# The second MLP's products as seven of quarters instead of eight, with the weights' sums formed during the first MLP

## The chip, the cores and the metric

The kernel runs on 1 core of one Trainium2 chip. The metric is device time in microseconds (us), the median of several executions. TensorE (PE) multiplies, VectorE (DVE), ScalarE (ACT) and GpSimd (POOL) do elementwise work, and SyncE (SP) issues the DMA transfers.

## The reference

```python
def _moe_ref(x, w_in, w_out, s, b):          # first MLP
    h = x @ w_in
    r = np.maximum(h, 0.0)
    return (s * (r * r) + b) @ w_out

def _moe2_ref(x, w_in, w_out):               # second MLP, beta = 1
    h = x @ w_in
    g = np.where(h >= 1, h, np.where(h <= -1, 0.0, (h + 1) ** 2 / 4))
    return g @ w_out

x = _attn_ref(q, k, v)   # 4 batches, 8 heads, 576 positions of 64; 4 heads local (32 back), 4 strided (every 32nd)
x = x.transpose(0, 2, 1, 3).reshape(2304, 512)
return _moe2_ref(_moe_ref(x, ...), ...)      # both MLPs: 512 -> 2048 -> 512
```

## The kernel before

Attention runs in 38 tiles (`attend`): scores on PE, mask and row maximum on DVE (L366), exponentials on ACT (L376), the division by the row sum (L383), a transpose (L392), the product with v (L404, L408). What it gives is written as a pair of tiles, `xh` (rounded to the matmul's type) and `xl` (the remainder).

Both MLPs are tiled alike. Tokens come in five units of 512, 448, 448, 448 and 448; the 2048 hidden rows in two halves (`hf`) of eight blocks of 128 (`m`). For each layer, half, unit and block, `hidden` multiplies four chunks of the input by a weight block into one PSUM bank `h`, and `output`, two steps later (`LAG`), adds four products into the PSUM banks `acc`. A step is thus 24 matmuls, since every product is done as three (`mm3`: high by high, high by low, low by high; L451 to L453). Between the two lies the nonlinearity, in the second MLP L487 (ACT), L488 and L490 (DVE), and the split of its result into `gh` (L258, ACT) and `gl` (L492, POOL). The sums of the first half go to DRAM (`part`) and come back for the second half.

Weights come as 64-bit floats, 512 KB for one of 64 blocks; four DVE instructions (L287 to L293) decode them, and L296 on POOL makes the low part. They lie in `w0h`, `w0l`, `w1h`, `w1l`, and six blocks of each layer's second half go into tiles that attention has left.

No engine decides the order at run time. `Issue.order` is a planner: it gives each operation a due time from back to front, and then takes the one that can start first on its costs, ties by due time. Operations with two possible engines have two entries; in the kernel before, DVE is charged 0.07 more there (`SPARE`). "port" in an entry keeps DVE and POOL from being planned at once.

## Time and profile before

| | us |
|---|---|
| median of 3 runs (910.68 to 911.11) | 911.03 |
| the profiled execution | 909.68 |
| its span, first to last instruction | 907.9 |
| PE busy in the span (98%) | 888.9 |
| first matmul of the first MLP | 33.57 |
| first matmul of the second MLP | 498.65 |
| last matmul starts | 903.76 |

The profiled execution lasted 1.78 us longer than its span. A matmul's busy time of 0.36 us overlaps its neighbours: the pace is read from start to start. The first 24 matmuls of 448 columns behind 498.65 still belong to the first MLP (its last two steps).

### The profile page before, as it was taken

What the parts mean: (1) busy time and instruction counts of PE and PEld (TensorE: products, weight loads), DVE (VectorE), ACT (ScalarE), POOL (GpSimd) and SP (SyncE); (2) the same over time, 40 slices, a digit from 0 to 9 for tenths busy, and PEclk for the clock granted to TensorE, in tenths of its full rate; (3) what the DMA queues carried; (4) which work ended last, traced back from release to release, by engine and by line L of the source; (5) the groups of instructions that cost most, each with busy time, mean ns of one, the idle gap of its engine ahead of it and who ended that gap; (6) DMA issues with size and microseconds to landing.
All of it is one profiled execution on the core that took longest, in us unless ns stands there. A gap on an engine that the chain in (4) does not pass through costs nothing.

```text
span 907.9 us, 12795 instructions
## 1 busy us (share of the span) xinstructions
PE 888.9 (98%) x4670; PEld 783.8 (86%) x4670; DVE 437.4 (48%) x990; ACT 411.3 (45%) x936; POOL 368.5 (41%) x329
## 2 busy tenths in 40 slices
PE   7899999999999999999999999999999999999998
PEld 4677789889989888999999888999999889999997
DVE  5988923333247676621147787233267523323232
ACT  6877745555445556544354445233244422222221
POOL 2565642333236656542446565222235422222221
PEclk9999999999999999999999999999999999999999
DMA  9666442322214433110303234011132102012021
GB/s 330 206 207 205 143 140 84 114 65 85 91 44 136 134 97 106 47 41 1 110 12 123 69 96 137 1 42 39 49 110 93 64 1 87 31 52 82 1 82 41
DMA packets 37502, 81.63 MB, mean 90 GB/s; under 512 B 4160, under 2 KB 19520, under 8 KB 37440
## 3 DMA queue, kind: packets, MB, share of 16 engines
q1 hardware_dynamic: 37440, 80.82, 27.8%
q8 instruction: 37, 0.61, 0.3%
q14 instruction: 25, 0.20, 0.1%
HBM read 66.64 MB, written 14.16 MB: 89 GB/s over the span
## 4 chain that ended last, share of the span: by engine, by line
PE 91%; ACT 3%; DVE 3%; POOL 1%; issue 1%; DMA 1%; SPq 0%; POOLq 0%; ACTq 0%
PE acc L451 15%; PE h L451 15%; PE h L452 14%; PE h L453 14%; PE acc L452 14%; PE acc L453 14%; ACT sm L376 2%; PE side L392 1%; PE side L357 1%; PE side L404 1%; PE side L408 1%; PE side L353 1%; DVE dt L293 1%; DMA w1h<-in_strd 1%; DVE sm L366 1%
## 5 line engine op out<-in xcount | busy, mean ns | idle before, releaser
L492 POOL TENSOR_TENSOR gl<-t,gh 128x448 fp32r<-128x448 f32 (+1 forms) x160 | 200.6, 1254 | 392.9 <-ACT gh L258 315.4
L451 PE MATMUL h<-xh,w0h 128*128 128x448 f32 (+1 forms) x460 | 175.5, 382 | 0.0
L451 PE MATMUL acc<-gh,w1h 128*128 128x448 f32 (+1 forms) x460 | 173.4, 377 | 0.5 <-ACT po L258 0.5
L452 PE MATMUL h<-xl,w0h 128*128 128x448 f32 (+1 forms) x460 | 171.2, 372 | 0.0
L453 PE MATMUL h<-xh,w0l 128*128 128x448 f32 (+1 forms) x460 | 171.1, 372 | 0.0
L452 PE MATMUL acc<-gl,w1h 128*128 128x448 f32 (+1 forms) x460 | 169.9, 369 | 0.0
L453 PE MATMUL acc<-gh,w1l 128*128 128x448 f32 (+1 forms) x460 | 169.7, 369 | 0.0
L258 ACT ACTIVATE gh<-t 128x448 fp32r<-128x448 f32 (+1 forms) x160 | 94.1, 588 | 139.8 <-DVE t L490 106.1
L488 DVE SCALAR_TENSOR_TENSOR t<-t 128x448 f32<-128x448 f32 (+1 forms) x80 | 54.9, 686 | 197.4 <-ACT t L487 197.3
L487 ACT ACTIVATE t<-h,half_t 128x448 f32<-128x448 f32 (+1 forms) x80 | 51.7, 646 | 148.4 <-PE h L453 148.3
L484 DVE TENSOR_SCALAR t<-t,fix_t 128x448 f32<-128x448 f32 (+1 forms) x80 | 51.0, 638 | 136.3 <-ACT t L479 118.2
L451 PEld LDWEIGHTS acc<-gh,w1h 128*128 128x128 f32 x460 | 86.3, 188 | 11.1 <-issue 1.0
L453 PEld LDWEIGHTS h<-xh,w0l 128*128 128x128 f32 x460 | 86.6, 188 | 10.5 <-POOL w0l L296 0.6
L451 PEld LDWEIGHTS h<-xh,w0h 128*128 128x128 f32 x460 | 86.7, 188 | 10.4 <-issue 0.5
L475 ACT ACTIVATE t<-h 128x448 f32<-128x448 f32 (+1 forms) x80 | 44.4, 555 | 112.5 <-PE h L453 111.4
L453 PEld LDWEIGHTS acc<-gh,w1l 128*128 128x128 f32 x460 | 86.2, 187 | 10.4
L452 PEld LDWEIGHTS h<-xl,w0h 128*128 128x128 f32 x460 | 86.8, 189 | 9.2
L452 PEld LDWEIGHTS acc<-gl,w1h 128*128 128x128 f32 x460 | 86.4, 188 | 8.5
L376 ACT ACTIVATE sm<-sm,mx 128x96 f32<-128x96 f32 (+2 forms) x152 | 56.1, 372 | 20.5 <-DVE mx L366 20.4
L293 DVE SCALAR_TENSOR_TENSOR dt<-raw,dt 128x512 int32<-128x512 int32 x64 | 64.0, 1003 | 0.6
L291 DVE SCALAR_TENSOR_TENSOR dt<-raw,dt 128x512 int32<-128x512 int32 x64 | 57.5, 898 | 0.6
L490 DVE TENSOR_TENSOR t<-h,t 128x448 f32<-128x448 f32 (+1 forms) x80 | 50.8, 635 | 2.0
(95 smaller groups left out, 1336.7 us busy)
## 6 DMA issues: line engine op xcount, KB each, us to landing
raw<-in_w_ins SPq DMA_DIRECT2D x32, 512.0 KB, 4.1
raw<-in_w_outs SPq DMA_DIRECT2D x32, 512.0 KB, 3.6
part<-po SPq DMA_DIRECT2D x32, 224.0 KB, 2.2
...
qv<-in_loc SPq DMA_DIRECT2D x18, 256.0 KB, 2.7
kb<-in_loc SPq DMA_DIRECT2D x15, 256.0 KB, 3.5
kb<-in_strd SPq DMA_DIRECT2D x15, 256.0 KB, 3.5
...
```

Source lines behind the costliest of these rows:

```text
L258: e.activation(out=out, in_=in_, func=AF.Copy)
L291: op(lambda e: e.scalar_tensor_tensor(out=t.tile, in0=words(1), scalar=-0x40000000, in1=t.tile, op0=ALU.bitwise_and, op1=ALU.bitwise_or), ...
L293: op(lambda e: e.scalar_tensor_tensor(out=t.tile, in0=words(0), scalar=29, in1=t.tile, op0=ALU.logical_shift_right, op1=ALU.bitwise_or), [ ...
L376: e.activation(out=sm.tile[0:nq, a, 0:nk], in_=sm.tile[0:nq, a, 0:nk], func=AF.Exp, scale=-1.0, bias=mx.tile[0:nq, a:a + 1], accum_out=dn. ...
L451: e.matmul(out=acc, lhsT=wh, rhs=ah, start=first, stop=False)
L452: e.matmul(out=acc, lhsT=wh, rhs=al, start=False, stop=False)
L453: e.matmul(out=acc, lhsT=wl, rhs=ah, start=False, stop=last)
L484: op(lambda e: e.tensor_scalar(out=c(t), in0=c(t), scalar1=sb_t[:, 0:1], scalar2=sb_t[:, 1:2], op0=MUL, op1=ADD), [dve2(n, 0.0007)], [fix_ ...
L487: op(lambda e: e.activation(out=c(t), in_=c(p), func=AF.Relu, scale=0.5, bias=half_t), [act(n)], [p], [t])
L488: op(lambda e: e.scalar_tensor_tensor(out=c(t), in0=c(t), scalar=1.0, in1=c(t), op0=ALU.min, op1=MUL), [dve2(n)], (), [t])
L490: op(lambda e: e.tensor_tensor(out=c(t), in0=c(p), in1=c(t), op=ALU.max), [dve(n)], [p], [t])
L492: op(lambda e: e.tensor_tensor(out=c(gl), in0=c(t), in1=c(gh).bitcast(F32), op=SUB), [pool(n)] + [dve2(n)], [t, gh], [gl])
```

## The change

The second MLP is no longer made of steps. Tokens come in three pairs of two 384-token tiles. A product of a weight matrix with a pair is taken as a 2 by 2 product of quarters: weights A11 to A22 (the contraction halved, the output halved), inputs B11 to B22 (the contraction halved, the two token tiles). Seven products (`PRODS`) of quarters or sums of quarters give the four results: weights A11, A12, A22 and S1 to S4, inputs B11, B21, B22 and T1 to T4.

The weights' sums are made once by `prepare` during the first MLP, 16 times: two 512 KB blocks are decoded, four sums of 256 columns formed, seven matrices split into high and low parts, and eight DMAs write these to DRAM (`dw`). Six of the 16 come in the first MLP's first half. In the second MLP every block loads one matrix (256 KB, `wmat`) and does six matmuls of 384 columns with it. `w0h` and `w0l` hold 16 such matrices.

For each pair, `inputs` forms T1 to T4 in place in the first MLP's output (`x2`, held in the freed `xh` tiles) and splits the seven inputs. `hidden2` does 4 groups of 14 blocks, each for two blocks of 128 hidden rows in both halves; products are added into banks that hold earlier ones, and `evacuate` copies or adds (L745) between them. Then come the nonlinearity (L758, L759, L761) and `output2`: for each of the seven products 8 blocks, whose input is a quarter of the nonlinearity's result or a sum made in place (L806) and is split just ahead into `gh` (ACT) and `gl` (L812), three buffers deep. Partial sums in DRAM are no longer needed in the second MLP.

The planner loses `SPARE`; now an entry is charged what it is slower than the operation's fastest engine. Attention's operations are pulled forward (`AHEAD`), and its loads, the weights' and others keep their order as lines.

```diff
--- before.py
+++ after.py
...
+AHEAD = 3.3
...
-BUFS = {"kb": KB, "qv": QV, "sm": SM, "pt": PT}
-SPARE_TAGS = [(("kb", "kb"), ("qv", "sm")), (("kb", "kb"), ("sm", "sm")), (("qv", "qv"), ("pt", "pt"))]
+BUFS = {"kb": KB, "qv": QV - 1, "qx": 1, "sm": SM - 1, "sx": 1, "pt": PT}
+SPARE_TAGS = {(0, 0): ("kb", "kb"), (0, 1): ("kb", "kb"), (1, 0): ("qx", "sx")}
...
+NP = 384
+PAIRS = NT // (2 * NP)
+KP = DFF // 256
+
+PRODS = ((1, "A11", "B11"), (5, "S1", "T1"), (6, "S2", "T2"), (3, "S4", "B22"), (7, "S3", "T3"), (2, "A12", "B21"),
+         (4, "A22", "T4"))
+WMAT = {"A11": 0, "A12": 1, "A22": 2, "S2": 3, "S4": 4, "S3": 5, "S1": 6}
+
+SUMS = {"T1": ("B11", "B12", "B11"), "T2": ("B11", "B22", "B11"), "T3": ("B12", "B22", "B12"), "T4": ("B21", "B21", "B11")}
+EARLY = 6
+CP = 9
+G_TAGS = ["kb"] * 4 + ["qv", "qv", "qx", "sx"] + ["sm"] * 2 + ["pt"] * 2 + ["pi"] * 4 + ["w1h", "w1l"] * 8
 SPACE_A, SPACE_W = 2.6, 2.4
-SPARE = 0.07
...
-                    key = (at + (SPARE if e == "dve" and len(o.engs) > 1 else 0.0), o.due, o.n, d, at)
+                    key = (at + d - min(x[1] for x in o.engs), o.due, o.n, d, at)
...
+    def prepare(o, i):
+
+        begin = len(plan.ops)
+        src = w_outs if o else w_ins
+        at = o * KP + i
+        tag = ("qv", "sm")[at % 2]
+        d1, d2 = (buf(sp, tag, [128, DM], I32, BUFS[tag]) for _ in range(2))
+        _, x1, _, load = decode(src[2 * MS + i], lasts if at < EARLY else [*lasts, chain[0]], [d1, d2], d1)
+        _, x2, *_ = decode(src[2 * MS + KP + i], [load], (), d2)
+        where = {"A11": (d1, x1, 0), "A22": (d2, x2, 1)}
+        where.update({"A21": (d1, x1, 1), "A12": (d2, x2, 0)} if o else {"A12": (d1, x1, 1), "A21": (d2, x2, 0)})
+
+        def parts(b, f, k, names):
+            n, q = 256 * len(names), [WMAT[name] for name in names]
+            qs = slice(q[0], q[-1] + 1, max(q[-1] - q[0], 1))
+            hi = buf(sp, "pt", [128, 512], F32R, PT)
+            lo = buf(sp, "pi", [128, 512], F32R, KD) if at < EARLY else buf(sp, "po", [128, 512], F32R, PO)
+            x = lambda: f()[:, k * 256:k * 256 + n]
+            op(lambda e: copy(e, hi.tile[:, 0:n], x()), [act(n)], [b], [hi], allocs=[lo],
+               line=pi_line if at < EARLY else None)
+            op(lambda e: e.tensor_tensor(out=lo.tile[:, 0:n], in0=x(), in1=hi.tile[:, 0:n].bitcast(F32), op=SUB),
+               [pool(n), dve2(n)], [b, hi], [lo])
+            for w, y in enumerate((hi, lo)):
+                op(lambda e, y=y, w=w: e.dma_start(
+                    out=dw[o][i][qs, :, w, :].rearrange("q p n -> p q n"),
+                    in_=y.tile[:, 0:n].bitcast(F32).rearrange("p (q n) -> p q n", n=256)), [dma(n * 512)], [y],
+                   part=[dw_buf[o][i][v] for v in q])
+
+        for names in [("A11",), ("A12", "A22")] if o else [("A11", "A12"), ("A22",)]:
+            parts(*where[names[0]], names)
+
+        for name, l, r, how in (("A22", "A21", "A22", ADD), ("A21", "A11", "A21", SUB), ("A11", "A22", "A11", SUB),
+                                ("A12", "A12", "A11", SUB)):
+            (b, f, k), (bl, fl, kl), (br, fr, kr) = (where[v] for v in (name, l, r))
+            h = lambda f, k: f()[:, k * 256:(k + 1) * 256]
+            op(lambda e, f=f, k=k, fl=fl, kl=kl, fr=fr, kr=kr, how=how: e.tensor_tensor(
+                out=h(f, k), in0=h(fl, kl), in1=h(fr, kr), op=how), [dve2(256), pool(256)],
+               [v for v in dict.fromkeys((bl, br)) if v is not b], [b])
+        for names in [("S2", "S3"), ("S4", "S1")] if o else [("S2", "S4"), ("S3", "S1")]:
+            parts(*((d1, x1) if names[0] == "S2" else (d2, x2)), 0, names)
+        prepared.extend(plan.ops[begin:])
...
+    def inputs(p):
+        t0 = {f"B{k}{t}": (2 * p + t - 1) * NP for k in (1, 2) for t in (1, 2)}
+        ks = lambda b: slice(0, 2) if b[1] == "1" else slice(2, 4)
+        x = lambda b, u, a, n: x2[u].tile[:, ks(b), a:a + n]
+        for i, (_, _, name) in enumerate(PRODS):
+            place = name
+            if name in SUMS:
+                place, l, r = SUMS[name]
+                cuts = sorted({0, NP} | {d for b in (place, l, r) for _, _, d, _ in span(t0[b], NP)})
+                todo = []
+                for c0, c1 in zip(cuts, cuts[1:]):
+                    f = {b: next(span(t0[b] + c0, c1 - c0))[:2] for b in {place, l, r}}
+                    todo.append((f, c1 - c0))
+
+                def sums(e, todo=todo, place=place, l=l, r=r):
+                    for f, n in todo:
+                        e.tensor_tensor(out=x(place, *f[place], n), in0=x(l, *f[l], n), in1=x(r, *f[r], n), op=SUB)
...
+                op(sums, [("dve", 0.07 * len(todo) + 2 * NP * 0.00104, 0.1, "port"),
...
+                whole = lambda w, d, n, b=b: b.tile[:, w, :, d:d + n]
+                hi = [lambda d=d, n=n, f=whole: f(0, d, n) for _, _, d, n in pieces]
+                lo = [lambda d=d, n=n, f=whole: f(1, d, n) for _, _, d, n in pieces]
+                n = len(pieces)
+                op(lambda e, src=src, hi=hi: [copy(e, h(), s()) for s, h in zip(src, hi)],
+                   [("act", 0.17 * n + 2 * NP * 0.00062, 0.1)], [quarter[p][place]], [b], after=[x_last[i], *prepared])
+                op(lambda e, src=src, hi=hi, lo=lo: [e.tensor_tensor(out=l(), in0=s(), in1=h().bitcast(F32), op=SUB)
+                                                     for s, h, l in zip(src, hi, lo)],
+                   [("pool", 0.1 * n + 2 * NP * 0.0022, 0.1, "port"), ("dve", 0.07 * n + 2 * NP * 0.00104, 0.1, "port")],
+                   [quarter[p][place]], [b])
             else:
-                got = x_buf[u][c]
-                op(lambda e, y=y, c=c: copy(e, xh[u][:, c, :], y.tile[:, 0:n]), [act(n)], [y], [got])
-                op(lambda e, y=y, c=c: e.tensor_tensor(out=xl[u][:, c, :], in0=y.tile[:, 0:n],
...
+    def wmat(o, i, name):
+        tag = ("w0h", "w0l")[loads[0] % 2]
+        loads[0] += 1
+        y = buf(wp, tag, [128, 2, 256], F32R, MS)
+        q = WMAT[name]
+        op(lambda e: e.dma_start(out=y.tile.bitcast(F32), in_=dw[o][i][q]), [dma(512 * 512)], [dw_buf[o][i][q]], [y], line=w_line,
+           after=() if w_line else w_loads)
+        return y
+
...
+    def evacuate(k, x, z, y, c, done):
+
+        if k == 1:
+            c["p1"] = place()
+            op(lambda e: copy(e, c["p1"].tile, x.tile), [act(n), dve(n)], [x], [c["p1"]], after=x0_free, line=c_line)
+        elif k == 5:
+            c["p5"] = place()
+            op(lambda e: copy(e, c["p5"].tile, z.tile), [act(n), dve(n)], [z], [c["p5"]], after=x0_free, line=c_line)
+        elif k == 6:
+            c["u2"] = place()
+            op(lambda e: copy(e, c["u2"].tile, x.tile), [act(n), dve(n)], [x], [c["u2"]], after=x0_free, line=c_line)
+        elif k == 4:
+            done("C21", x)
+        else:
+            s, d, what = {3: (z, c.get("u2"), "C12"), 7: (x, c.get("p5"), "C22"), 2: (y, c["p1"], "C11")}[k]
+            op(lambda e: e.tensor_tensor(out=d.tile, in0=s.tile, in1=d.tile, op=ADD), [dve(n)], [s], [d])
+            done(what, d)
+
+    gq = {}
...
+        in_psum = what == "C21"
+        op(lambda e: e.activation(out=t.tile, in_=c.tile, func=AF.Relu, scale=0.5, bias=half_t), [act(n)], [c], [t])
+        op(lambda e: e.scalar_tensor_tensor(out=t.tile, in0=t.tile, scalar=1.0, in1=t.tile, op0=ALU.min, op1=MUL),
+           [dve2(n)], (), [t])
+        op(lambda e: e.tensor_tensor(out=t.tile, in0=c.tile, in1=t.tile, op=ALU.max),
+           [dve(n)] if in_psum else [dve2(n)], [c], [t])
...
+    def hidden2(p):
+        for i0 in range(0, KP, 2):
+            x, z, y = banks()
+            cs = [{}, {}]
+            for k, a, b in PRODS:
+                for s in range(2):
+                    i = i0 + s
+                    dst = {1: x, 6: x, 7: x, 4: x, 5: z, 3: z, 2: y}[k][s]
+                    w = wmat(0, i, a)
+                    bufs, at = tmats[p, b]
+
+                    def f(e, dst=dst, w=w, at=at, k=k):
+                        for j in range(2):
+                            wj = [w.tile[:, v, j * 128:(j + 1) * 128] for v in range(2)]
+                            mm3s(e, dst.tile, wj, (at(0, j), at(1, j)), k in START, j == 0, j == 1)
+
+                    pe_block(f, [w, *bufs], [dst])
+                for s in range(2):
+                    evacuate(k, x[s], z[s], y[s], cs[s], lambda what, c, i=i0 + s: nonlinear(p, i, what, c))
+
...
+    def output2(p):
+        x, z, y = banks()
+        cs = [{}, {}]
+        for k, a, b in PRODS:
+            dst = {1: x, 6: x, 7: x, 4: x, 5: z, 3: z, 2: y}[k]
+            for i in range(KP):
+                home = b
+                if b in SUMS:
+                    home, l, r = SUMS[b]
+                    d, l, r = (gq[p, i, v] for v in (home, l, r))
+                    op(lambda e, d=d, l=l, r=r: e.tensor_tensor(out=d.tile, in0=l.tile, in1=r.tile, op=SUB),
+                       [dve2(n), pool(n)], [v for v in (l, r) if v is not d], [d])
+                g = gq[p, i, home]
+                hi = buf(sp, "gh", [128, n], F32R, LAG + 1)
+                lo = buf(sp, "gl", [128, n], F32R, LAG + 1)
+                op(lambda e, g=g, hi=hi: copy(e, hi.tile, g.tile), [act(n)], [g], [hi], allocs=[lo], line=g_line)
+                op(lambda e, g=g, hi=hi, lo=lo: e.tensor_tensor(out=lo.tile, in0=g.tile, in1=hi.tile.bitcast(F32), op=SUB),
+                   [pool(n), dve2(n)], [g, hi], [lo])
+                w = wmat(1, i, a)
+
+                def f(e, dst=dst, w=w, hi=hi, lo=lo, k=k, i=i):
+                    for c in range(2):
+                        wc = [w.tile[:, v, c * 128:(c + 1) * 128] for v in range(2)]
+                        mm3s(e, dst[c].tile, wc, (hi.tile, lo.tile), k in START, i == 0, i == KP - 1)
+
...
+                o.sooner = AHEAD * max(at - MS, 0)
...
+    slots = {(1, u, m): 1 for u, ms in ((1, (0, 3, 6)), (2, (0, 2, 4, 6)), (3, (0, 2, 4))) for m in ms}
+    slots[0, NU - 1, 0] = EARLY
+    for hf, u, m in steps:
+        g = hf * MS + m
+        if hf == m == 0:
...
+        for _ in range(slots.get((hf, u, m), 0)):
+            prepare(*todo.pop(0))
+    assert not todo
     while pend:
         output(*pend.pop(0))
+    x0_free = []
+    for p in range(PAIRS):
+        a = len(plan.ops)
+        inputs(p)
+        if p == 0:
+            x0_free += plan.ops[a:]
+        hidden2(p)
+        output2(p)
     plan.spaced(starts, SPACE_A)
     plan.spaced(decodes, SPACE_W)
 
```

Three places in the order of the engines. TensorE, output product of the second MLP, before: one block of hidden rows, four `acc` banks in turn (two shown).

```order
L451 MATMUL acc_1045_5738<-gh_5863,w1h_5027 128x448
L452 MATMUL acc_1045_5738<-gl_5864,w1h_5027 128x448
L453 MATMUL acc_1045_5738<-gh_5863,w1l_5028 128x448
L451 MATMUL acc_1046_5746<-gh_5863,w1h_5027 128x448
L452 MATMUL acc_1046_5746<-gl_5864,w1h_5027 128x448
L453 MATMUL acc_1046_5746<-gh_5863,w1l_5028 128x448
```

After, `output2`: `w0h`, `w0l` are loaded matrices, `acc` the two banks of the product.

```order
L770 MATMUL acc_1209_6395<-gh_6389,w0l_6210 128x384
L771 MATMUL acc_1209_6395<-gl_6390,w0l_6210 128x384
L772 MATMUL acc_1209_6395<-gh_6389,w0l_6210 128x384
L770 MATMUL acc_1210_6396<-gh_6389,w0l_6210 128x384
L771 MATMUL acc_1210_6396<-gl_6390,w0l_6210 128x384
L772 MATMUL acc_1210_6396<-gh_6389,w0l_6210 128x384
L770 MATMUL acc_1209_6395<-gh_6404,w0h_6223 128x384
L771 MATMUL acc_1209_6395<-gl_6405,w0h_6223 128x384
L772 MATMUL acc_1209_6395<-gh_6404,w0h_6223 128x384
```

A weight matrix now serves two banks of 384 columns and then the next one with the next `gh`, `gl` comes.

GpSimd in the second MLP's last part, before: nothing but the low parts.

```order
L492 TENSOR_TENSOR gl_6890<-t_6888,gh_6889 128x448
L492 TENSOR_TENSOR gl_6923<-t_6921,gh_6922 128x448
L492 TENSOR_TENSOR gl_6958<-t_6956,gh_6957 128x448
L492 TENSOR_TENSOR gl_7005<-t_7003,gh_7004 128x448
L492 TENSOR_TENSOR gl_7042<-t_7040,gh_7041 128x448
```

VectorE in `output2`, after: low parts (L812) and the sums in place (L806), mostly in turn.

```order
L812 TENSOR_TENSOR gl_6376<-kb_5732,gh_6375 128x384
L806 TENSOR_TENSOR w1l_6024<-w1l_6048,w1l_6024 128x384
L812 TENSOR_TENSOR gl_6390<-qv_5738,gh_6389 128x384
L806 TENSOR_TENSOR kb_5732<-kb_5699,kb_5732 128x384
L812 TENSOR_TENSOR gl_6405<-sm_5909,gh_6404 128x384
L806 TENSOR_TENSOR qv_5738<-sx_5720,qv_5738 128x384
L806 TENSOR_TENSOR sm_5909<-pt_5876,sm_5909 128x384
L812 TENSOR_TENSOR gl_6424<-pi_5915,gh_6423 128x384
```

The low parts have moved from GpSimd to VectorE; of 168 in the second MLP, 164 are there, and 95 of the 96 sums.

GpSimd in attention, before: division by the row sums (L383) and low parts of weights (L296).

```order
L383 TENSOR_TENSOR sm_348<-sm_348,dn_350 128x4x96
L380 TENSOR_SCALAR dn_385<-dn_385 128x4
L383 TENSOR_TENSOR sm_383<-sm_383,dn_385 128x4x96
L380 TENSOR_SCALAR dn_439<-dn_439 128x4
L383 TENSOR_TENSOR sm_437<-sm_437,dn_439 128x4x96
L296 TENSOR_TENSOR w0l_312<-dt_420,w0h_311 128x512
L296 TENSOR_TENSOR w0l_345<-dt_452,w0h_344 128x512
```

VectorE in attention, after: the same divisions are L461, between decodes (L300 to L306) and reciprocals.

```order
L460 RECIPROCAL dn_360<-dn_360 128x4
L304 SCALAR_TENSOR_TENSOR dt_288<-raw_194,dt_288 128x512
L461 TENSOR_TENSOR sm_358<-sm_358,dn_360 128x4x96
L460 RECIPROCAL dn_392<-dn_392 128x4
L306 SCALAR_TENSOR_TENSOR dt_288<-raw_194,dt_288 128x512
L461 TENSOR_TENSOR sm_390<-sm_390,dn_392 128x4x96
L458 TENSOR_SCALAR dn_431<-dn_431 128x4
L460 RECIPROCAL dn_431<-dn_431 128x4
L518 TENSOR_TENSOR xl_77<-side_459,xh_72 128x2x128
L461 TENSOR_TENSOR sx_429<-sx_429,dn_431 128x4x96
L300 TENSOR_SCALAR dt_492<-dt_492 128x512
```

Of 38 divisions 33 are on VectorE now, of the 32 low parts of weights 30, of the first MLP's 80 `gl` 78. Ahead of the eighth L560 (the first unit's last hidden block) VectorE has 21 divisions, 13 low parts of weights, 6 `gl`, and 23 of the 38 tiles' masks (24 in the kernel before, at its eighth L484).

## Rows read from the trace of the kernel before

**Rows 1.** Page, parts 1 and 2: busy us of the span; granted clock in tenths, 40 slices.
```profile
PE 888.9 (98%) x4670; PEld 783.8 (86%) x4670; DVE 437.4 (48%) x990; ACT 411.3 (45%) x936; POOL 368.5 (41%) x329
PEclk9999999999999999999999999999999999999999
```
**Rows 2.** Windows: stretch, length, busy us (x instructions) by engine, PEclk, DMA share, GB/s.
```profile
0.00:107.00 107.00, 92.22 (x639) 69.23 (x640) 88.77 (x349) 79.36 (x281) 56.87 (x66) 0.98 0.70 227
107.00:503.80 396.80, 396.34 (x2113) 354.49 (x2112) 173.42 (x375) 200.00 (x436) 179.19 (x159) 1.00 0.27 84
498.60:903.97 405.37, 405.37 (x1946) 364.60 (x1944) 176.74 (x271) 134.37 (x224) 135.00 (x107) 1.00 0.18 58
```
**Rows 3.** Timeline, TensorE: start us, us, instruction; streaming matmuls of the second MLP.
```profile
709.36 0.39 PE L451 MATMUL h<-xh,qv 128*128 128x512 f32 x1
...
742.30 0.40 PE L453 MATMUL acc<-gh,w1l 128*128 128x512 f32 x1
...
752.97 0.37 PE L451 MATMUL h<-xh,qv 128*128 128x448 f32 x1
...
903.76 0.37 PE L453 MATMUL acc<-gh,w1l 128*128 128x448 f32 x1
```
**Rows 4.** Timeline, weight loads of TensorE in attention: start us, us, load, count.
```profile
58.71 0.97 PEld L357 LDWEIGHTS side<-kb,kb 128*128 128x128 f32 x8 [0.75 <-DVE mx L366]
```
**Rows 5.** Timeline, a hidden step of the second MLP: PE, then ACT and DVE after it.
```profile
603.80 0.37 PE L453 MATMUL h<-xh,w0l 128*128 128x448 f32 x1
...
604.26 0.64 ACT L487 ACTIVATE t<-h,half_t 128x448 f32<-128x448 f32 x1 [2.34 <-PE h L453]
...
604.93 0.63 DVE L488 SCALAR_TENSOR_TENSOR t<-t 128x448 f32<-128x448 f32 x1 [3.62 <-ACT t L487]
...
605.59 0.62 DVE L490 TENSOR_TENSOR t<-h,t 128x448 f32<-128x448 f32 x1
```
**Rows 6.** Timeline and groups by shape, VectorE: neighbours overlap; means by width.
```profile
520.32 0.68 DVE L490 TENSOR_TENSOR t<-h,t 128x512 f32<-128x512 f32 x1
520.92 0.68 DVE L291 SCALAR_TENSOR_TENSOR dt<-raw,dt 128x512 int32<-128x512 int32 x1
521.63 0.69 DVE L293 SCALAR_TENSOR_TENSOR dt<-raw,dt 128x512 int32<-128x512 int32 x1
...
L490 DVE TENSOR_TENSOR t<-h,t 128x448 f32<-128x448 f32 x64 | 39.9, 623 | 1.8
L490 DVE TENSOR_TENSOR t<-h,t 128x512 f32<-128x512 f32 x16 | 11.0, 686 | 0.2
L440 DVE TENSOR_TENSOR xl<-side,xh 128x256 fp32r<-128x256 f32 x16 | 6.7, 421 | 9.8 <-ACT xh L258 9.7
```
**Rows 7.** One line's instructions, VectorE decode: min/median/max ns; then the same by mean.
```profile
L291 DVE SCALAR_TENSOR_TENSOR dt<-raw,dt x64: 654/686/1780, 28.9 to 720.1; 128x512 int32<-128x512 int32 x64
L293 DVE SCALAR_TENSOR_TENSOR dt<-raw,dt x64: 675/688/1787, 30.6 to 720.9; 128x512 int32<-128x512 int32 x64
...
L293 DVE SCALAR_TENSOR_TENSOR dt<-raw,dt 128x512 int32<-128x512 int32 x64 | 64.0, 1003 | 0.6
L291 DVE SCALAR_TENSOR_TENSOR dt<-raw,dt 128x512 int32<-128x512 int32 x64 | 57.5, 898 | 0.6
```
**Rows 8.** Groups by shape, GpSimd and ScalarE, as before.
```profile
L492 POOL TENSOR_TENSOR gl<-t,gh 128x448 fp32r<-128x448 f32 x128 | 154.7, 1209 | 343.2 <-ACT gh L258 284.4 <-issue 44.8 <-PE side L392 4.6
L383 POOL TENSOR_TENSOR sm<-sm,dn 126x504 f32<-126x504 f32 x16 | 17.3, 1082 | 8.4 <-DVE dn L382 4.2 <-ACT t L479 1.4 <-ACT sm L376 1.3
...
L258 ACT ACTIVATE gh<-t 128x448 fp32r<-128x448 f32 x128 | 73.9, 577 | 117.9 <-DVE t L490 86.3 <-DVE t L484 31.2
```
**Rows 9.** Windows: DMA share and GB/s last; then a DMA issue of the page (KB, us).
```profile
10.00:20.00 10.00, 8.14 (x66) 6.04 (x65) 7.75 (x49) 7.78 (x39) 4.52 (x7) 1.00 1.06 390
22.70:45.40 22.70, 19.39 (x180) 14.51 (x174) 22.33 (x80) 18.59 (x65) 12.19 (x15) 1.00 0.67 206
...
kb<-in_strd SPq DMA_DIRECT2D x15, 256.0 KB, 3.5
```

237 lines of the change are left out of this document (174 added, 63 removed).

## The prediction

> **What bounds the kernel now.** I read the page's busy times first, then stretches, then single instructions. TensorE is busy 98% of the span and its clock stands at the upper of its two levels, 2.4 GHz, in all 40 slices [rows 1]. In the second MLP's stretch it is busy all of the 405.37 us, while VectorE has 176.7 us of work and the DMA engines 18% of their time [rows 2]. So there the number of matmuls and their pace set the time, and nothing else ends last. Only in the first 107 us does TensorE stand: 92.2 us busy, and VectorE, with 88.8 us, is nearly as full [rows 2].
>
> The pace: 144 matmuls of 512 columns start from 709.36 to 742.30, 143 intervals of 0.2303 us; 744 of 448 columns start from 752.97 to 903.76, 743 intervals of 0.2030 us [rows 3]. The line through both has 0.428 ns a column, and gives 0.1756 us at 384. With 0.4167 ns a column (2.4 GHz) the surplus is 0.017 us at 512 and 0.0163 at 448, and 384 would take 0.177. I take 0.176.
>
> **Products.** Before, the second MLP has 1920 matmuls: 384 x 0.2303 + 1536 x 0.2030 = 400.2 us. After, it has 3 pairs x 112 blocks x 6 = 2016 of 384 columns: 2016 x 0.176 = 354.8 us, between 353.9 and 356.8 by the two extrapolations. So 45.4 us go, all of it on the path, since the stretch has no idle time. The last matmul would start at 903.76 - 45.4 = 858.4, and with the 4.1 us from there to the end of the span (907.9 - 903.76; the last copy and store stay) the span would be 862.5 if nothing new waits.
>
> **Can the weights be loaded into the array so fast?** Eight loads of 128 x 128 in attention take 0.97 us together, the last one 0.19 of it, so they follow each other at 0.11 us [rows 4]. A load every 0.176 us is slower than that, and costs nothing.
>
> **The matrices' transfers.** A block of six matmuls lasts 1.056 us and needs 256 KB: 248 GB/s, 88.1 MB in all, where this stretch moved 58 GB/s [rows 2]. From 10 to 20 us the queue moved 390 GB/s, with transfers of up to 512 KB [rows 9]. A single 256 KB transfer lands in 3.5 us [rows 9], and the 16 buffers let it start up to 16.9 us ahead. Taken as hidden. If that cover were gone the second MLP would run at the supply's rate (first rival).
>
> **VectorE in the second MLP.** An instruction of 512 columns takes 0.686 us, one of 256 0.421: 0.156 + 1.035 ns a column, so 0.553 at 384; neighbours without a dependence overlap by 0.08 (0.68 long, 0.60 from start to start), dependent ones stand 0.03 apart [rows 6]. Before has no subtraction with both inputs and result in SBUF on VectorE; these rows are the nearest, and I keep 0.473 to 0.583 for it. A pair has 88 instructions of 384 columns in `hidden2` and 94 in `output2`, 182 x 0.473 = 86.1 us, and some 21 pieces of `inputs` with 8448 columns, 10.4 us: 96.5 of the pair's 118.3 us of TensorE. With the next pair's inputs `output2` alone holds 54.9 of 59.1 us. It fits, but barely there. At 0.583 it would be 106 + 12.7 = 119 a pair, just TensorE's own time.
>
> **The hand-over in `output2`.** Three buffers of `gh` and `gl`: block b+3 may be split when block b is done, two blocks (2.11 us) before it is needed. From the last matmul's start at 603.80 ACT starts 0.46 us later, which is 0.26 after the next matmul could start; VectorE starts 0.03 after ACT ends [rows 5]. With 0.53 us of ACT at 384 (0.577 at 448 [rows 8]), 0.55 of VectorE and some 0.1 to TensorE (an estimate, as such gaps are in rows 5) that is 1.47 us, 0.64 short of the window; one sum (0.47) in front of it still fits, two do not. Where VectorE has two sums or a piece of `inputs` in a row, I expect waits of a few tenths. For both things together I add 4 us, from 0 to 20.
>
> **The first MLP, after attention.** Its matmuls are the same. What is added for the sums hides under them if VectorE has room from 107 to 503.8 us, the 396.8 us in which TensorE is full [rows 2]. By the order it has there 48 decodes of four, 61 low parts and 17 of the weights (at most 0.61 each, 165 us), 63 sums of 256 columns (0.34, 21 us), 72 `gl`, 72 scalings, 20 adds and 13 squares (0.54, 96 us) and the last 15 attention tiles, at most 88.8 / 24 = 3.7 each, 56 us: 338 us at most. It fits. The 128 writes (29.4 MB) add some 75 GB/s to 84; in order on SP they may hold a load behind them, which had 27% of the time filled. Zero, and up to 4 us at the joint: the last low part of the sums stands one hidden step ahead of the first input, and a late write would show there. I add 1.
>
> **Attention.** VectorE takes over 21 divisions (0.52), 13 low parts of weights and 6 `gl` (0.61) ahead of the first unit's end: 22.5 us more on 88.8. Against that GpSimd no longer disturbs it: L291 and L293 have medians of 686 and 688 ns but means of 898 and 1003 [rows 7], and 16 decodes give back at least 16 x 0.53 = 8.4 us. That makes 103 of 107 us. The chain itself gets shorter, since a division took 1.08 us on GpSimd [rows 8] and about 0.6 here. If VectorE keeps its 18.2 us of idle time, the stage ends 14 us later; if the shorter chain decides, some 5 of TensorE's 14.8 idle us go. I add 4.
>
> **Sum.** 862.5 + 4 + 1 + 4 = 871.5 us of span. The profiled execution lasted 1.8 us longer than its span, and the median is 1.35 above it: 874.6, so 875 us.
>
> **Rivals.** (1) The supply of matrices sets the pace. Place: `w0h` and `w0l`, the wait of each block's first matmul. Under 88.1 MB / 400 us = 220 GB/s, a little less with what else is added, the gain is gone. At the 206 GB/s of 22.7 to 45.4 us [rows 9] the second MLP takes 428 us, and the time is 948: slower. Against it: that slice had the DMA engines filled to 67% only, so the kernel asked for no more. The Trainium skill, DMA: Bandwidth & Descriptors, section Bandwidth, speaks for this rival: it asks for transfers of 1 MiB and more, and has 0.95 us for 64 KB and 6.15 for 1 MB; between them 256 KB would take 1.99 us (an estimate from that page), 336 of them 669 us, and the time would be some 1190 us. The 390 GB/s of rows 9 contradict it as long as transfers overlap. 3%.
>
> (2) The change doesn't do what it says: narrow matmuls are not cheaper, as a load takes 0.19 us [rows 4] and would have to end before the next begins. 2016 x 0.2015 = 406 us, and the time is 926, slower too. The 0.11 us spacing is against it. 2%.
>
> (3) Hand-over: each of 168 `output2` blocks waits 0.1 to 0.2 us because a sum or an input stands ahead of its low part. 17 to 34 us in place of 4: 888 to 905. For it: 54.9 of 59.1 us, and the order has sums in pairs. 13%.
>
> (4) VectorE bounds attention: 14 us and more in place of 4, 885 to 890. For it: 103 of 107 us. 13%.
>
> (5) Attention gets shorter and nothing waits: 861 to 866. 6%.
>
> **How the numbers follow.** The forecast, 866 to 885, has 62%, (5) 6%, (4) 13%, (3) 13%, (1) and (2) 5%; 1% falls within 0.2%. About 0.2% is what a measurement of this kernel can tell from no change. The range reaches from 863, through the forecast and (4), into most of (3): 863 to 894. Faster 94%, same 1%, slower 5%.
>
> **What would show it.** In the profile after: 2016 matmuls 0.176 us apart in the second MLP; DMA at about 250 GB/s there with no wait of PE on a DMA; VectorE busy some 85% in that stretch and GpSimd nearly idle; PE's waits in `output2` of tenths, on VectorE; PE idle in the first 110 us within 10 to 30 us. Intervals of 0.20 us, or PE waiting for `dw` loads, would make it wrong, and so would waits of whole microseconds where products are added into a bank that is still being copied.

## The result: 872.5 us, and where the time is in the profile after

The changed kernel takes 872.54 us (median of four runs, 869.2 to 873.9) beside 910.86 for the kernel before: a ratio of 0.957, with an interval of 0.9555 to 0.959. The forecast was 875, range 863 to 894. The profiled execution lasted 872.55 us, its span 870.3; the forecast for these two was 873.3 and 871.5.

Page of after, parts 1 and 2 (busy us by engine; granted clock in tenths over 40 slices), which answers [rows 1]:

```profile
PE 848.7 (98%) x4766; PEld 782.1 (90%) x4766; DVE 690.0 (79%) x1709; ACT 506.5 (58%) x1153; POOL 30.2 (3%) x46
PEclk7699999999999999999999999999999999999999
```

Windows of after, with the columns of [rows 2]: until 107 us, the rest of the first MLP, the second MLP.

```profile
0.00:107.00 107.00, 93.50 (x598) 71.95 (x599) 92.44 (x371) 76.94 (x259) 11.60 (x24) 0.87 0.65 213
107.00:510.10 403.10, 402.12 (x2154) 359.45 (x2153) 303.17 (x730) 231.14 (x513) 10.80 (x17) 1.00 0.60 193
510.10:866.60 356.50, 352.73 (x2017) 350.73 (x2016) 293.83 (x609) 198.14 (x383) 7.77 (x5) 1.00 0.80 249
```

The second MLP shrank from 400.4 us (498.65 + 24 matmuls of 0.203 to 903.76) to 356.5 and is still nearly full of TensorE's work. It has 609 instructions of VectorE (293.8 us, 82%), five of GpSimd, and 249 GB/s of transfers. It starts at 510.1 instead of 503.5. Two things here were not forecast: the granted clock is low in the first two of the 40 slices, and 3.8 us of the last window are without work of TensorE. TensorE's waits in that window are these two (us in total, times, longest):

```profile
PE side L770 <- ACT cpx L282: 3.4, 1, 3.4
PE acc L770 <- DVE x L606: 0.3, 1, 0.3
```

None is on a transfer, and no wait of the profile is in an output half. The second MLP is six halves, hidden and output of three pairs, 336 matmuls each; from one's first matmul to the next one's they last 64.16, 59.01, 58.25, 58.58, 58.25 and 58.40 us. The timeline of TensorE at the third half (first and last matmul) gives the undisturbed pace, 335 intervals in 58.08 us, 0.1734 us each, where 0.176 was taken:

```profile
633.29 0.33 PE L770 MATMUL h<-tm,w0h 128*128 128x384 f32 x1
...
691.37 0.33 PE L772 MATMUL side<-raw,w0l 128*128 128x384 f32 x1
```

The first half has 5.9 us more than the third. Timeline of after at the joint, where the second MLP follows the first, TensorE and then ScalarE:

```profile
514.73 0.34 PE L772 MATMUL acc<-tm,w0l 128*128 128x384 f32 x1
518.50 0.45 PE L770 MATMUL side<-tm,w0h 128*128 128x384 f32 x1 [3.43 <-ACT cpx L282]
...
519.70 0.53 PE L770 MATMUL side<-tm,w0l 128*128 128x384 f32 x1
520.02 0.53 PE L771 MATMUL side<-tm,w0l 128*128 128x384 f32 x1
```

```profile
505.33 0.83 ACT L282 ACTIVATE tm<-x 128x768 fp32r<-128x768 f32 x1
...
513.20 0.84 ACT L282 ACTIVATE tm<-x 128x768 fp32r<-128x768 f32 x1 [2.11 <-DVE x L636]
515.53 0.84 ACT L282 ACTIVATE raw<-x 128x768 fp32r<-128x768 f32 x1 [1.49 <-DVE x L636]
517.95 0.49 ACT L282 ACTIVATE cpx<-side 128x384 f32<-128x384 f32 x1 [1.57 <-DVE dt L679]
```

The first product's bank (`side`) is free for the third product only when it is copied to `cpx`; that copy waits for all seven inputs of pair 0 (the list `x0_free`), and these are split one after the other from 505.33 to 517.9 us, behind the last low part of the weights' sums at 500.35. For the first 1.1 us after the wait the matmuls start some 0.18 us apart, and from 519.70 on 0.32, where their pace is 0.1734: the clock has gone to 1.2 GHz. It is 0.98 in the mean from 510 to 520 us and 0.85 from 520 to 530, which makes 3.4 us at that level.

The same on a larger scale stands at the start. Windows of before and of after, 10 to 40 us (the first of before is in [rows 9]):

```profile
20.00:30.00 10.00, 8.97 (x114) 7.41 (x116) 9.01 (x52) 8.94 (x41) 4.99 (x9) 1.00 0.73 246
30.00:40.00 10.00, 9.07 (x67) 6.80 (x64) 9.93 (x29) 7.63 (x26) 5.52 (x6) 1.00 0.80 246
```

```profile
10.00:20.00 10.00, 7.64 (x38) 5.59 (x37) 9.15 (x43) 7.50 (x27) 0.22 (x1) 0.67 1.05 393
20.00:30.00 10.00, 8.06 (x48) 6.33 (x47) 8.13 (x40) 7.02 (x29) 3.11 (x4) 0.67 0.52 182
30.00:40.00 10.00, 8.94 (x69) 7.27 (x70) 7.19 (x38) 7.41 (x30) 0.44 (x2) 0.50 0.32 86
```

The column behind the engines is the mean granted clock: 1.00 is 2.4 GHz, 0.50 is 1.2. Before, it is 1.00 in all three; after, TensorE runs at 1.2 GHz for most of these 30 us, so its busy time there is worth less. The first matmul of the first MLP comes at 44.26 us instead of 33.57. And the runs of after follow their mean clock: 869.2 us at 0.992, 872.54 at 0.986, 872.55 at 0.982, 873.9 at 0.978.

### The profile page after: what moved, and what is told of

The parts are those of the page before. It is cut to its first block, busy times and chain, and to the rows that moved or that the text cites. A ratio compares the mean times of both kernels' runs of the same rounds, so it can differ in the third digit from the quotient of the medians.

```text
span 870.3 us, 14705 instructions
## 1 busy us (share of the span) xinstructions
PE 848.7 (98%) x4766; PEld 782.1 (90%) x4766; DVE 690.0 (79%) x1709; ACT 506.5 (58%) x1153; POOL 30.2 (3%) x46
## 4 chain that ended last, share of the span: by engine, by line
PE 93%; DVE 4%; ACT 1%; DMA 1%; issue 0%; SPq 0%; ACTq 0%
PE h L529 8%; PE h L530 8%; PE h L531 8%; PE acc L529 7%; PE acc L530 7%; PE acc L531 7%; PE acc L771 6%; PE acc L770 6%; PE acc L772 6%; PE side L771 4%; PE side L770 4%; PE side L772 4%; PE h L771 3%; PE h L770 3%; PE h L772 3%; PE side L431 1%
## 5 line engine op out<-in xcount | busy, mean ns | idle before, releaser
L529 PE MATMUL acc<-gh,w1h 128*128 128x448 f32 (+1 forms) x300 | 114.7, 382 | 0.9 <-ACT po L282 0.9
L531 PE MATMUL acc<-gh,w1l 128*128 128x448 f32 (+1 forms) x300 | 110.7, 369 | 0.0
L530 PE MATMUL acc<-gl,w1h 128*128 128x448 f32 (+1 forms) x300 | 110.5, 368 | 0.0
L529 PE MATMUL h<-xh,w0h 128*128 128x448 f32 (+1 forms) x280 | 108.1, 386 | 0.0
L530 PE MATMUL h<-xl,w0h 128*128 128x448 f32 (+1 forms) x280 | 104.4, 373 | 1.0 <-DVE xl L518 1.0
L531 PE MATMUL h<-xh,w0l 128*128 128x448 f32 (+1 forms) x280 | 104.2, 372 | 0.0
L560 DVE TENSOR_SCALAR t<-t,fix_t 128x448 f32<-128x448 f32 (+1 forms) x80 | 41.6, 521 | 49.4 <-ACT t L555 49.2
L282 ACT ACTIVATE gh<-t 128x448 fp32r<-128x448 f32 (+1 forms) x80 | 46.9, 586 | 34.3 <-DVE t L560 33.9
L563 DVE TENSOR_TENSOR gl<-t,gh 128x448 fp32r<-128x448 f32 (+1 forms) x78 | 49.5, 634 | 11.9 <-ACT gh L282 8.2
L530 PEld LDWEIGHTS h<-xl,w0h 128*128 128x128 f32 x280 | 52.6, 188 | 6.8 <-DVE xl L518 1.3
L555 ACT ACTIVATE t<-t 128x448 f32<-128x448 f32 (+1 forms) x66 | 39.0, 591 | 1.6
L812 DVE TENSOR_TENSOR gl<-w1h,gh 128x384 fp32r<-128x384 f32 x60 | 32.9, 551 | 6.7 <-ACT gh L282 6.7
L745 DVE TENSOR_TENSOR cpx<-acc,cpx 128x384 f32<-128x384 f32 x33 | 18.1, 553 | 18.9 <-PE acc L772 18.7
```

Of the source, the lines that this page charges most:

```text
L282: e.activation(out=out, in_=in_, func=AF.Copy)
L529: e.matmul(out=acc, lhsT=wh, rhs=ah, start=first, stop=False)
L530: e.matmul(out=acc, lhsT=wh, rhs=al, start=False, stop=False)
L531: e.matmul(out=acc, lhsT=wl, rhs=ah, start=False, stop=last)
L555: e.activation(out=c(t), in_=c(t), func=AF.Square)
L560: op(lambda e: e.tensor_scalar(out=c(t), in0=c(t), scalar1=sb_t[:, 0:1], scalar2=sb_t[:, 1:2], op0=MUL, op1=ADD), [dve2(n, 0.0007)], [fix_ ...
```

## The experiments

Theories: the saving is the count of matmuls at the pace of their width; what is lost is lost at two places, the joint (inputs that wait without need) and the start (a low clock). Rivals: VectorE, which took over GpSimd's work, bounds the start; and VectorE or the supply of matrices is level with TensorE in the second MLP. Medians are of four runs where no other number stands; the kernel before took 911.0 to 911.8 us beside each group.

### Is the saving the number of matmuls?

```
  # in hidden2 and output2, behind the block of product k
+ if k == 2: pe_block(again, ...)      # the same six matmuls once more
```

> The kernel after with the block of six matmuls of product 2 done twice (its sum in the bank counts double, so the output differs in the second MLP): eight products of 384 columns again, 2304 matmuls instead of 2016, and no other work on any engine, no other transfer. Theory A (the number of matmuls times their pace sets the second MLP's time): 288 x 0.1734 us = 50 us more, 921 to 924 us, slower than the kernel before. Theory B (something else, VectorE or the matrices' transfers, is level with TensorE there and sets the pace): part of the added work hides beside it, 890 to 915 us.

921.72 us (two runs), 49.2 more than after: 288 matmuls more at 0.1734 us are 49.9. In the profiles an undisturbed half lasts 66.6 us instead of 58.25. The added blocks hid beside nothing, and the time is 1.1% above that of the kernel before (ratio 1.007 to 1.016), whose eight products it then has again. Leaving out one product in eight is thus worth all that the count says, and TensorE bounds the second MLP.

```
- UNITS = [512, 448, 448, 448, 448]    # in the kernel before
+ UNITS = [384] * 6
```

> The kernel before with the tokens cut into six tiles of 384 instead of one of 512 and four of 448; both MLPs in eight products, 4608 matmuls of 384 columns instead of 768 of 512 and 3072 of 448. This measures the pace at 384 columns apart from the seven products. Theory A (the pace of 0.1734 us in the kernel after is that of the width): undisturbed stretches of the first and second MLP run at 0.173 to 0.174 us a matmul, both MLPs take 799 us instead of 800.5, and the time is 908 to 914 us. Theory B (the straight line through 448 and 512 columns holds, 0.176, and the kernel after is quicker for another reason, such as its order of the weights): 0.1755 to 0.177 us a matmul, and 919 to 925 us.

Timeline of this kernel, TensorE: 1151 intervals without a disturbance.

```profile
357.51 0.34 PE L451 MATMUL h<-xh,kb 128*128 128x384 f32 x1
...
557.98 0.34 PE L453 MATMUL acc<-gh,w1l 128*128 128x384 f32 x1
```

200.47 / 1151 = 0.1742 us. So 0.173 to 0.174 is the pace of that width, in the structure of before too, and the straight line through [rows 3] missed it by some 0.002. The time, 934.01 us (two runs, ratio 1.025), was forecast by neither: before 357.5 us this kernel starts 1344 matmuls of 384 columns, 234 us at their pace, in 321 us. Attention's matmuls lie between them there, but TensorE also stands for 18.6 of the 321 us, where the kernel before stands for 7.9 from the start of its first MLP to 357.5; the longest of these waits are for low parts and rounded copies of weights (3.8 and 3.2 us). Why they come late was not followed up.

### The joint

```
  # the first five inputs of a pair (those in the T tiles)
- [quarter[p][place]], [b], after=[x_last[i], *prepared])
+ [quarter[p][place]], [b], after=[x_last[i]])
```

> The first five inputs of each pair (the tiles in the first MLP's space) no longer wait until all sums of the weights are made, so that pair 0's may be split while the first MLP still runs; the order of the rest follows from it. Theory A (the whole-microsecond waits at 513.75 and 518.50 us come from the copies of the first products, which stand on ScalarE behind five inputs split between 506 and 518 us): the 3.43 us wait of TensorE on the copy goes, the intervals of 0.32 us behind it go too, the first half of the second MLP takes 59 us instead of 64.2, and the time falls by 4 to 6 us, to 866.5 to 868.5. Theory B (what is late at the joint is the last of the weights' sums or VectorE's work as such): the work moved forward delays the first MLP by what is won behind it, and the time stays at 871 to 873.

867.35 us, ratio 0.951 (0.947 to 0.954). In its profile the first half lasts 58.24 us and TensorE has no wait at all in the second MLP. Timeline of ScalarE at the joint of this kernel: the copy stands at 512.98, where it stood at 517.95.

```profile
510.90 0.85 ACT L282 ACTIVATE raw<-x 128x768 fp32r<-128x768 f32 x1 [3.68 <-DVE x L636]
512.98 0.49 ACT L282 ACTIVATE cpx<-side 128x384 f32<-128x384 f32 x1 [1.24 <-DVE dt L679]
513.71 0.49 ACT L282 ACTIVATE cpx<-acc 128x384 f32<-128x384 f32 x1 [0.24 <-PE acc L772]
```

Five of the seven inputs are split from 358.65 us on. The second MLP starts at 510.39, where it was 510.12, but its first MLP starts 2.5 us sooner; in the pair of kernels below whose clocks are nearly alike it starts at 505.90 with the early inputs and at 506.75 without. So the inputs split earlier did not delay the first MLP there. Theory A holds: the joint was a matter of order, not of VectorE's work as such. The half was forecast at 59 and came at its undisturbed 58.24.

### The start: the gap behind the warm-up

After issues a 512 KB load of weights second; the first scores wait 2.27 us for theirs, until 6.18 us (4.39 before).

```
- WARM = 6
+ WARM = 12
```

> Twelve warm-up matmuls instead of six; nothing else differs. They end near 6.5 us, where the kernel after starts its first scores at 6.18 after 2.27 us without work. Theory A (the 2.27 us in which TensorE stands at the start is why the granted clock falls to 1.2 GHz from 8.8 to 42 us, and the lower clock is what stretches attention from 33.6 to 44.3 us): the granted clock stays at 2.4 GHz through the first 45 us, the first matmul of the first MLP comes near 38 instead of 44.26, the second MLP starts 3 to 6 us sooner than at 510.1, and the whole takes 867 to 870 us. Theory B (VectorE bounds the first 107 us, and TensorE's clock there only follows its low load): the clock may change, the start of the second MLP does not move by more than 1 us, and the time stays at 872 to 873 us.

870.44 us, with an interval of the ratio (0.952 to 0.958) that overlaps that of after. In windows of 1 us the clock of after stands at 1.2 GHz from 7.6 to 11 us, and again from 14.4; with the gap bridged the first fall is gone, but not the second, at 13.8 us. The second MLP starts at 509.68. The runs span 868.41 (clock 0.994) to 873.38 (0.984).

The clock column has to be read with care at the start: it counts the time before the clock's first record as 2.4 GHz (e_joint has 1.00 there from 0 to 10 us). The warm-up matmuls of 512 columns start 0.43 us apart in every kernel, the later fillers of that width 0.22, and the scores of e_joint and, below, of e_warm_fill_joint show the same two paces (twelve in 5.46 us, four in 1.03):

```profile
6.14 5.46 PE L431 MATMUL acc<-w1l,w1h 128*126 128x256 f32 x12 [2.23 <-DMA w1h<-in_strd]
```

```profile
6.98 1.03 PE L436 MATMUL acc<-w1l,w1h 128*126 128x256 f32 x4
```

So every kernel starts at 1.2 GHz. By the first record it comes to 2.4 at 4.2 us in after, at 7.0 in e_warm and only at 12.1 in e_joint. Up to the second fall after thus has 4.2 + 3.4 us at the lower level and e_warm 7.0: the longer warm-up changed the order of these and hardly their sum.

```
  # in emit: the first load of weights behind the next loads of attention
+ ops.insert(sp[5], ops.pop(sp[1]))
```

> The first transfer of the first MLP's weights (512 KB) is issued sixth instead of second, behind the transfers of the first two attention tiles and half of the constants; nothing else differs. Theory A (this transfer delays the first scores from 4.39 to 6.18 us, and the gap after the warm-up lowers the clock): the first scores start near 4.5 to 5.2 us, the gap behind the warm-up shrinks to about 1 us, the clock stays high longer, and the time falls by 2 to 6 us, to 867 to 870. Theory B (VectorE bounds the first 107 us): the first scores start earlier, the second MLP starts at 509 to 510 us as before, and the time stays within 1.2 us of 872.5.

873.03 us. The first scores start at 4.32 us behind a gap of 0.41, but the wait has only moved to a later pair of loads, and the clock is 0.50 from 10 to 20 us. Timeline of TensorE in this kernel:

```profile
4.32 1.78 PE L434 MATMUL acc<-w1l,w1h 128*126 128x256 f32 x4 [0.41 <-DMA w1h<-in_strd]
6.49 1.10 PE L434 MATMUL acc<-w1l,w1h 128*126 128x256 f32 x4 [0.39 <-DMA w1h<-in_strd]
10.60 2.07 PE L434 MATMUL acc<-w1l,w1h 128*126 128x256 f32 x4 [3.01 <-DMA w1h<-in_strd]
```

So the first gap explains the first fall at most, and 0.4 us of the second MLP's start; theory A falls in both runs. Theory B, that the clock only follows VectorE, is taken up below. Both edits of e_warm and e_joint together:

```
- WARM = 6
+ WARM = 12
- ... after=[x_last[i], *prepared])
+ ... after=[x_last[i]])
```

> Both edits: twelve warm-up matmuls, and the first five inputs without the wait for the weights' sums. If both causes are real and separate, the gains add: 3 to 5 us from the start and 4 to 6 us at the joint, 861.5 to 865.5 us. If VectorE bounds the first stretch and only the joint is real, 866.5 to 868.5; if neither, 872.

863.5 us (861.27 to 866.27), by the sum expected; but its four runs again go with their clock (0.994, 0.994, 0.99 and 0.984 in order of time), so what it has over e_joint is not shown to be the warm-up's. Its profiled execution, the one of 861.27, starts the second MLP at 504.64 us, sooner than any other kernel with the change, with the clock at 0.66 from 10 to 20 us and at 0.83 from 30 to 40: the start does not follow the clock alone.

### The start: clock, or VectorE?

```
  # in attend, the tiles ahead of the first unit's end
+ for _ in range(2 * early): fill(e, sc.tile, 128, 512)       # in scores
+ for _ in range(2 * early): fill(e, tp.tile, nk, 4 * nq)     # in flip
```

> The kernel of e_joint with 36 matmuls of zeros (bf16, up to 512 columns, some 0.21 us each at the upper clock) put in front of the scores and the transposes of the first attention tiles, into banks that these overwrite; they end before the first matmul of the first MLP. They do nothing for the result and cost TensorE some 7.7 us of work before that point. Theory A (TensorE's clock at 1.2 GHz in attention is what the time follows from one execution to the next, e_joint's four runs going from 863.06 at a mean clock of 0.996 to 869.71 at 0.984): the granted clock stays at 2.4 GHz in the first 45 us, the first MLP starts at or before 40 us instead of 41.7, the mean clock is 0.995 or more in every run, and all runs lie within 1.5 us of each other near 861 to 863. Theory B (the low clock is a sign of waiting for VectorE and costs nothing): the clock rises, the start of the second MLP stays at 510 us, the time at 866 to 870, or some us more for the added work.

863.03 us, 4.3 less than e_joint, with 36 matmuls more, though the intervals of the two ratios overlap (0.944 to 0.951 and 0.947 to 0.954). The clock is 0.996 to 0.999; the spread, 861.34 to 866.09, is wider than forecast. With the longer warm-up as well:

```
- WARM = 6        # in e_fill_joint
+ WARM = 12
```

> The kernel of e_fill_joint (first five inputs without the wait for the weights' sums, 36 matmuls of zeros in attention) with twelve warm-up matmuls instead of six, so that TensorE's longest wait at the start goes too. Theory A (time at the lower clock in the first 50 us is what makes the runs of one kernel differ): mean clock 0.996 or more in all runs, median 861 to 863 us. Theory B (the fillers already gave what there is, and twelve warm-up matmuls only move the first scores by 0.2 us): 863 us as before, with the same spread of 861.3 to 866.1.

862.28 us, 861.53 to 863.44: mean clocks of 0.999 and three times 1.0, and the spread of 6.65 us of e_joint is down to 1.9. Windows of this kernel and, below, of e_joint:

```profile
10.00:20.00 10.00, 8.09 (x59) 5.30 (x58) 9.70 (x46) 8.96 (x33) 0.22 (x1) 1.00 1.04 383
30.00:40.00 10.00, 7.54 (x92) 5.26 (x91) 9.74 (x38) 7.74 (x22) 0.16 (x1) 1.00 0.75 230
```

```profile
10.00:20.00 10.00, 7.79 (x40) 5.14 (x39) 9.42 (x43) 8.02 (x30) 0.22 (x1) 0.83 1.03 376
30.00:40.00 10.00, 7.83 (x85) 6.04 (x84) 8.65 (x31) 7.35 (x24) 0.22 (x1) 0.63 0.59 187
```

VectorE is as full in the one as in the other or fuller, and does more where the clock stays up (46 and 38 instructions instead of 43 and 31), though the edits gave work to TensorE alone: the lower clock held it back, not the other way round. The ratio of e_warm_fill_joint, 0.946 (0.944 to 0.948), lies below that of after without overlap; this version beats both kernels. Over e_warm_joint, which has no fillers and 863.5 us (0.945 to 0.951), it has no gain clear of noise: what the fillers are shown to do is to keep the clock up and the runs together. The same fillers and warm-up with the joint left as in after:

```
- ... after=[x_last[i]])        # in e_warm_fill_joint
+ ... after=[x_last[i], *prepared])
```

> The kernel after with the twelve warm-up matmuls and the 36 matmuls of zeros in attention, but with the wait at the joint left as it is in after (the first five inputs behind all sums of the weights). Theory A (start and joint are two separate losses that add): the clock stays at 2.4 GHz through attention, the second MLP starts at 505.5 to 506.5 us, its first half takes 64 us and the others 58.2 to 59.1, and the time is 868 us (866.5 to 869.5): 4 to 5 less than after, 5.9 more than e_warm_fill_joint. Theory B (the slow clock and the late joint share a cause, so that the joint is shorter when TensorE comes to it at an undisturbed clock): the first half takes 60 to 62 us and the time is 864 to 866.

869.09 us, 6.8 above e_warm_fill_joint; the first half lasts 65.08 us, the second MLP starts at 506.75. Theory A holds: start and joint are separate losses. Alone the edits for them take 3.5 and 5.2 us off after, and both together 10.3; by the intervals the 3.5 alone is not clear of noise.

```
- key = (at + d - min(x[1] for x in o.engs), o.due, o.n, d, at)
+ spare = 0.07 * (e == "dve" and len(o.engs) > 1) if at < 110.0 else d - min(...)
+ key = (at + spare, o.due, o.n, d, at)
```

> The kernel of e_joint with the old rule for the choice of the engine (GpSimd where it is free sooner) for everything that the planner puts into the first 110 us: divisions, small additions and low parts go back to GpSimd there (93 instructions on it instead of 52), the rest as in e_joint. Theory A (what stretches attention is VectorE: in the kernel after it does in the first 107 us 92.4 us of work and GpSimd 11.6, before 88.8 and 56.9): the first matmul of the first MLP comes at 34 to 37 us instead of 41.7, the second MLP starts at 503 to 506 instead of 510.4, and the time is 861 to 863. Theory B (TensorE's clock, not the engine choice, is what was lost): the first MLP starts at 40 us or later unless the granted clock stays high, VectorE's instructions beside GpSimd get longer (means of 0.9 to 1.0 us instead of 0.68 for the decoding's long ones), and the time stays at 865 to 870.

The first MLP starts at 36.35 us, as theory A has it, and the second at 512.2, as theory B; 867.45 us, the time of e_joint. GpSimd works 56.8 us of the first 107 and VectorE 79.9, so VectorE is relieved, but TensorE is not done sooner: the last matmul of the first half's 512-token tile starts at 146.0 us instead of 136.5, with more of attention in front of it. (The 129.4 and 116.4 named in the next expectation are starts of earlier matmuls of that tile.) VectorE's long decode instructions had means of 0.71 us there, not the 0.9 to 1.0 named, with GpSimd as busy as in before.

With the old rule for a shorter time, and the fillers:

```
- spare = ... if at < 110.0 else ...
+ spare = ... if at < 45.0 else ...        # on top of e_fill_joint
```

> The kernel of e_fill_joint with the old rule for the choice of the engine in the first 45 us of the plan alone, where GpSimd takes divisions and low parts again (70 instructions on it instead of some 50); behind that the rule of the kernel after. In e_pool110_joint the first MLP began at 36.35 us, but the 512-token tile took until 129.4 instead of 116.4. Theory A (sharing with GpSimd helps where the first scores and the first weights are waited for, and harms behind it): the first MLP starts at 34 to 37 us, the second MLP at 504 to 506 instead of 508.1, the time is 859 to 861.5. Theory B (TensorE's work in the first 310 us is the same whatever comes first, so that an earlier first MLP only moves attention behind it): the second MLP starts at 507 to 509, the time is 862 to 865.

863.79 us (861.62 to 865.49), the first MLP at 37.12, the second at 505.35: no gain over e_fill_joint in the time, though the profiled execution has the start of theory A. With the clock up, who divides is worth nothing that these runs can show. The rival that VectorE bounds the start is not borne out.

### How much room has VectorE in the output halves?

```
  # in output2, behind the low part
+ if b not in SUMS: op(<the same low part again>, [dve2(n)], [g, hi], [lo])
```

> The kernel of e_joint with the low part of the hidden values made a second time in 24 of the 56 blocks of each output half (products 1, 3 and 2, whose input is no sum): 72 instructions of VectorE more, each 0.55 us long and 0.47 us from the one before, 11.3 us in each of three halves that last 59 us and in which VectorE has 53 us of work. Theory A (VectorE fits the output halves only barely, and its room counts by halves): 53 + 11.3 = 64.3 us in 59, so each of the three halves gets some 5 us longer, in waits of TensorE for the low part, and the time is 877 to 884 us beside 867.4 of e_joint. Theory B (its room counts by pairs, since the queue runs ahead into the next hidden half with its 10 us of room): the intervals that are too long grow from some 0.28 us to 0.5 at the few blocks with two sums, and the time is 867 to 870 us.

883.47 us (two runs), 16.1 more than e_joint; its second MLP starts 4.5 us sooner. The hidden halves stay at 58.24 to 58.27, the output halves go from 58.80, 59.14 and 58.39 to 67.03, 67.62 and 62.75 us: 21 us for 72 instructions, 0.29 each, at the upper end of theory A. The longest of the waits, TensorE and then VectorE's queue in front of it:

```profile
592.48 0.45 PE L771 MATMUL acc<-gl,w0h 128*128 128x384 f32 x1 [1.03 <-DVE gl L815]
```

```profile
590.48 1.01 DVE L655 TENSOR_TENSOR tm<-x,tm 128x512 fp32r<-128x512 f32 x2
591.41 0.55 DVE L812 TENSOR_TENSOR gl<-sx,gh 128x384 fp32r<-128x384 f32 x1
591.88 0.55 DVE L815 TENSOR_TENSOR gl<-kb,gh 128x384 fp32r<-128x384 f32 x1
592.35 0.55 DVE L815 TENSOR_TENSOR gl<-sx,gh 128x384 fp32r<-128x384 f32 x1
```

A piece of the next pair's inputs (L655) stands in front of a low part, as the prediction describes it. In the kernel after such pieces stand there too, but VectorE gets through its queue in time. The room counts by halves, and it is less than the 11 us added to each.

## The prediction, step by step

**What bounds it, and the count.** Right: TensorE, full in the second MLP but for the one wait at the joint, 2016 matmuls; shown by e_eight.

**Pace.** Mis-sized: 0.1734 to 0.1742 us, not 0.176, below both extrapolations. The step that failed took a straight line in columns, or a constant surplus over 2.4 GHz, from 448 and 512 columns; the surplus is 13 to 14 ns at 384 where it was 16 to 17. The products cost 349.5 us instead of 354.8: 5.3 us to the good.

**Loads and transfers.** Right: with a load every 0.173 us the array streams on, and the matrices came at 249 GB/s with no wait (rival 1 had 948 us, rival 2 926; its 0.2015 us a matmul follows from no line shown). Issues of after (count, KB, median us to landing):

```profile
w0h<-dw SPq DMA_DIRECT2D x168, 256.0 KB, 3.2
w0l<-dw SPq DMA_DIRECT2D x168, 256.0 KB, 3.1
```

Each takes 3.2 us and one is needed every 1.06 us, so about three are under way. The Trainium skill, DMA: Bandwidth & Descriptors, section Bandwidth, has times of transfers issued from GpSimd, by size; SyncE issues them here. 336 went through in 356.5 us and not in the 669 that the prediction estimated from that page one behind the other, so the measurement decides for overlap.

**VectorE.** Right in size: a pair has 48.24 + 52.36 us in the halves of e_joint, 100.6 of 117 (96.5 of 118.3 was forecast), instructions 0.55 long and 0.47 apart. Also right that GpSimd no longer disturbs it. Groups of after by shape (busy us, mean ns), the lines of [rows 7]:

```profile
L304 DVE SCALAR_TENSOR_TENSOR dt<-raw,dt 128x512 int32<-128x512 int32 x32 | 21.9, 684 | 0.3
L306 DVE SCALAR_TENSOR_TENSOR dt<-raw,dt 128x512 int32<-128x512 int32 x32 | 21.7, 682 | 0.1
```

They had means of 898 and 1003 ns; the other 32 of each line in after have 686 to 756. The Trainium skill, Trainium Architecture — The Big Picture, section What this means for kernel authors, says that the two engines share a pair of ports which one of them holds alone at a time; these rows agree with it. What the price is stays open: in the first 110 us of before, 24 decodes (L291, L293) that overlap an instruction of GpSimd have a mean of 1.02 us and the six others 0.68, but in e_pool110_joint the 16 that overlap one have 0.72. That GpSimd works at the same time is not enough to lengthen them.

**Hand-over.** The mechanism was right and the size too large: the three output halves together have 1.2 us over three times 58.25, not 4. Rival 3 (17 to 34 us) is out as the kernel stands; in e_dve24_joint, with 24 instructions more a half, it is there, 4.4 to 8.5 us a half. Where between the two it begins was not run.

**First MLP and joint.** The step that failed: "a late write would show there. I add 1." It was not a write but the order behind the sums: the inputs of pair 0, all behind the last sum, and the copies behind all inputs. It cost 5.9 us, by e_joint. The whole-microsecond wait on a bank still being copied, listed as what would make the forecast wrong, did occur, once.

**Attention.** With the rest of the first MLP 6.6 us (510.1 against 503.5), forecast 4, and by another way than forecast. VectorE had 92.4 us of work in the first 107, not 103, and TensorE stood for 13.5 us, within the 10 to 30 named. What was lost goes with TensorE's clock: with it at 2.4 GHz from 6.8 us on the second MLP starts at 505.9 (e_warm_fill_joint), 2.4 us behind 503.5, with 42 matmuls more. That is 4.2 of the 6.6 us, in one profile of each kernel; e_warm_joint at 504.64, with a lower clock and no fillers, shows that it is not a strict rule. That "its clock stands at the upper of its two levels" was read of before and carried over to the changed kernel without a term. (Nor does it quite hold of before: its warm-up runs at 1.2 GHz too, and the mean of its first 107 us is 0.98 [rows 2].) Rivals 4 and 5 were both built on VectorE alone.

**Sum.** Against the forecast, -5.3 for the pace, +6.6 + 5.9 - 5 for start and joint, 1.2 - 4 for the hand-over and -0.4 at the end make -1.0: 870.5, where the span was 870.3. The other 1.3 us of the difference to the forecast's 875 come from the step from span to median: 1.35 us were added because the median before lay above the profiled execution, and here it does not. The forecast was good to 0.3% by luck, because errors of 5 and 7 us in its terms cancelled.
